# Unsplit transposes and paired K columns in the first stage, another order of the first Q results, and a buffer of its own for the last block's transposes

## The chip, the cores and the metric

The kernel runs on one core of one Trainium2 chip. The core has a matrix engine (TensorE, PE in the profile), three engines for elementwise work (VectorE or DVE, ScalarE or ACT, GpSimd or POOL), a queue engine (SyncE or SP) that issues most transfers, and 16 DMA engines. The metric is the device time of one execution in microseconds. Of the kernel before, three runs were timed; their median is 664.66 us (663.19 to 666.59).

## The reference

Both branches read the same normalised input `xn`, with 2048 tokens and 512 channels. One is attention with 32 heads of 16 channels, the other a feed-forward over the token axis.

```python
def _A_ref(x, wqkv, wo):                    # B, S, D = 1, 2048, 512
    H = 32; Dh = D // H
    qkv = (x @ wqkv).reshape(B, S, 3, H, Dh).transpose(2, 0, 3, 1, 4)
    q, k, v = qkv[0], qkv[1], qkv[2]
    p = softmax(einsum("bhqd,bhkd->bhqk", q, k) * Dh ** -0.5)
    o = einsum("bhqk,bhkd->bhqd", p, v)
    return o.transpose(0, 2, 1, 3).reshape(B, S, D) @ wo

def _B_ref(x, w1, b1, w2, b2):              # F = 1376
    h = layernorm(x)
    u = gelu(einsum("bsd,sf->bdf", h, w1) + b1)
    y = einsum("bdf,fs->bds", u, w2) + b2
    return y.transpose(0, 2, 1)

xn = layernorm(x)
return x + _A_ref(xn, A_wqkv, A_wo) + _B_ref(xn, B_w1, B_b1, B_w2, B_b2)
```

## The kernel before

**A schedule made on the host.** Python code builds one ordered list of instructions for each engine before anything runs (class `Sched`, line 170). `Sched.add` takes an instruction with the data that it reads and writes, finds what it depends on, and gives it a planned start from a planned duration (`occ`, how long it holds its engine; `lat`, until its result may be read). `plan` turns dependencies into semaphore waits and `emit` writes the lists out. So the durations in the code (`TABLE`, `occ`, `lat`) do nothing on the chip themselves; they decide the order.

**The work.** Attention is cut into 32 blocks (4 quarters of the queries times 8 sets of 4 heads), and each block into 16 groups, one for each 128 keys: 512 groups. A group has four score matmuls, one per head, each 32 rows high, so that they run side by side in the array (`score_mm`, line 675). Its exponentials are made in one of two ways. Either ScalarE does it, two tiles of 128x1024 per group (`exp_tile`, line 700), or VectorE and GpSimd do it: VectorE copies the four score banks out as 16-bit integers (`dve_first`, line 760), and two shifted planes are added by VectorE or GpSimd (`add_plane`, line 773; `add_plane_pool`, line 779). PV, the product with the values (`pv_mm`, line 707), takes one set of four matmuls for a ScalarE group and three for a VectorE group. After a block, its sums are copied out, the denominators go through DRAM and come back as reciprocals spread over the partitions in `denb`, and GpSimd multiplies (`chain_epi`, line 1279). The projections, the feed-forward and the output product fill the time between scores as "chains" of steps on one PSUM bank each.

**The dispatcher** (line 1947 on) walks through planned time, and at each free engine picks the next step. `pe_step` issues the scores of the next ScalarE tile when one of its two double banks is free, and otherwise a PV set, a chain step or a filler matmul on zeros (line 1815). Its thresholds come from `POLICY` (line 97), one row of 16 numbers for each 10 us of planned time: how long scores may wait for other work, when VectorE gets a group, how full a bank queue must be, a seed that varies some of these, and so on.

**Form of the matmuls.** `mm` (line 604) issues a matmul whole while `quad[0]` is false; from line 1942 on, when the dispatcher runs, it splits each into four pieces of 32 output rows. That holds for transposes too (`turn=True`, line 610), which multiply a tile by the identity.

**The first stage.** x is loaded tile by tile (16 tiles of 128 tokens), normalised, transposed (`transpose_mm`, line 794) and copied to `xnT` (`xnT_evac`, line 822). Tiles 0 to 3 are written out by hand (lines 844 to 878) with the first Q (`qt0_mm`, `qt_evac`) and K (`k_mm`, `k_evac`); the others come as chains `chain_tp`, `chain_k1`, `chain_k`, `chain_v`. K for the first heads is multiplied tile by tile, 128 columns each. The query tile `QT` exists twice (slot 0 and 1), masked by `qmask`, in pieces of 256, 128 and 128 columns.

**The end.** The last block does not go through DRAM. `tail_epilogue` (line 1979) transposes its sums in 32x32 blocks on VectorE into `denb`, takes reciprocals, multiplies, and transposes back into `otmp`; then TensorE adds the last part of the output product to four banks (`tail["steps"]`, line 1418, holds what each bank still needs), and ScalarE and VectorE copy the results out for the store.

Of the kernel before, what the change touches and what calls it, by code (L numbers as in the profile page):

```python
# [66 lines left out]
class Op:  # L67
# [31 lines left out]
    (85.0, 140.0, 500.0, -1, 0, 1300.0, 100.0, 0.1, 3, 4, 2, 8500.0, 0, 0.0, 1200.0, 0),  # L99
    (175.0, 80.0, 500.0, -1, 0, 2000.0, 0.0, 0.2, 1, 5, 2, 8500.0, 18089, 0.0, 700.0, 2),  # L100
    (130.0, 150.0, 300.0, -1, 0, 1300.0, 0.0, 0.05, 2, 3, 2, 7500.0, 0, 0.0, 1000.0, 2),
    (205.0, 170.0, 450.0, -1, 0, 1300.0, 0.0, 0.05, 2, 3, 2, 10500.0, 93902, 1.0, 1800.0, 1),
    (185.0, 120.0, 350.0, -1, 0, 1300.0, 100.0, 0.2, 3, 3, 2, 5500.0, 0, 1.0, 1000.0, 2),
    (85.0, 140.0, 350.0, -1, 1, 1300.0, 100.0, 0.05, 3, 4, 0.9, 8000.0, 0, 0.0, 900.0, 1),
    (110.0, 230.0, 250.0, -1, 0, 1300.0, 0.0, 0.1, 1, 5, 2, 7500.0, 0, 150.0, 1000.0, 0),
    (85.0, 170.0, 350.0, 1, 0, 1300.0, 0.0, 0.05, 1, 3, 2, 7500.0, 0, 0.0, 800.0, 2),
    (115.0, 140.0, 300.0, -1, 0, 1300.0, 0.0, 0.2, 2, 3, 2, 5500.0, 57197, 1.0, 1000.0, 1),
    (195.0, 230.0, 250.0, 1, 0, 900.0, 0.0, 0.2, 3, 3, 2, 9500.0, 7708, 0.0, 700.0, 2),
    (140.0, 90.0, 400.0, -1, 1, 2000.0, 0.0, 0.2, 2, 5, 2, 7000.0, 0, 150.0, 700.0, 1),
    (85.0, 160.0, 300.0, -1, 0, 1300.0, 100.0, 0.1, 1, 4, 2, 5500.0, 0, 1.0, 1000.0, 1),  # L110
    (205.0, 150.0, 500.0, -1, 0, 900.0, 0.0, 0.1, 2, 5, 2, 8000.0, 35383, 150.0, 800.0, 1),
    (105.0, 130.0, 450.0, -1, 0, 2000.0, 200.0, 0.1, 2, 5, 0.9, 7000.0, 0, 1.0, 1200.0, 2),
    (130.0, 150.0, 300.0, -1, 0, 1300.0, 0.0, 0.05, 2, 3, 2, 7500.0, 0, 0.0, 1000.0, 2),
    (135.0, 230.0, 500.0, -1, 0, 900.0, 0.0, 0.05, 3, 3, 2, 6500.0, 0, 0.0, 1200.0, 1),
    (135.0, 230.0, 500.0, -1, 0, 900.0, 0.0, 0.05, 3, 3, 2, 6500.0, 0, 0.0, 1200.0, 1),
    (110.0, 110.0, 400.0, 1, 0, 2000.0, 0.0, 0.2, 2, 4, 2, 5500.0, 0, 0.0, 900.0, 2),
    (110.0, 190.0, 300.0, 1, 0, 900.0, 0.0, 0.05, 2, 4, 2, 5500.0, 61002, 150.0, 1000.0, 1),
    (135.0, 90.0, 350.0, 1, 0, 2000.0, 100.0, 0.05, 2, 5, 0.9, 5500.0, 0, 1.0, 1100.0, 2),
    (135.0, 90.0, 350.0, 1, 0, 2000.0, 100.0, 0.05, 2, 5, 0.9, 5500.0, 0, 1.0, 1100.0, 2),
    (135.0, 90.0, 350.0, 1, 0, 2000.0, 100.0, 0.05, 2, 5, 0.9, 5500.0, 0, 1.0, 1100.0, 2),  # L120
    (190.0, 230.0, 300.0, -1, 0, 1300.0, 0.0, 0.05, 1, 3, 2, 8000.0, 78883, 1.0, 1000.0, 0),
    (200.0, 220.0, 350.0, 1, 0, 900.0, 0.0, 0.0, 1, 3, 2, 10500.0, 0, 0.0, 800.0, 1),
    (170.0, 80.0, 300.0, -1, 0, 2000.0, 0.0, 0.05, 1, 2, 2, 8000.0, 42439, 1.0, 700.0, 2),
    (140.0, 90.0, 300.0, -1, 0, 2000.0, 0.0, 0.0, 1, 3, 2, 8500.0, 0, 0.0, 800.0, 1),
    (110.0, 180.0, 200.0, -1, 1, 1300.0, 200.0, 0.2, 1, 4, 2, 7000.0, 96947, 150.0, 500.0, 1),
    (110.0, 180.0, 200.0, -1, 1, 1300.0, 200.0, 0.2, 1, 4, 2, 7000.0, 96947, 150.0, 500.0, 1),
    (110.0, 180.0, 200.0, -1, 1, 1300.0, 200.0, 0.2, 1, 4, 2, 7000.0, 96947, 150.0, 500.0, 1),
    (95.0, 80.0, 500.0, 1, 0, 900.0, 0.0, 0.2, 1, 3, 2, 9500.0, 12616, 0.0, 1000.0, 1),
    (105.0, 210.0, 300.0, -1, 0, 1300.0, 0.0, 0.05, 2, 3, 2, 5500.0, 30810, 1.0, 1200.0, 2),
    (145.0, 240.0, 200.0, -1, 0, 1300.0, 100.0, 0.2, 1, 3, 2, 6500.0, 0, 0.0, 1200.0, 2),  # L130
    (130.0, 150.0, 300.0, -1, 0, 1300.0, 0.0, 0.05, 2, 3, 2, 7500.0, 0, 0.0, 1000.0, 2),
    (185.0, 170.0, 250.0, -1, 0, 2000.0, 0.0, 0.05, 2, 3, 2, 7500.0, 39811, 0.0, 1100.0, 2),
    (150.0, 160.0, 300.0, 1, 0, 2000.0, 200.0, 0.05, 2, 2, 2, 7500.0, 28503, 0.0, 1000.0, 2),
    (155.0, 170.0, 500.0, -1, 0, 900.0, 100.0, 0.2, 1, 4, 0.9, 6500.0, 0, 0.0, 500.0, 2),
    (170.0, 210.0, 300.0, -1, 1, 1300.0, 0.0, 0.05, 2, 5, 0.9, 8000.0, 0, 0.0, 1100.0, 1),
    (170.0, 130.0, 200.0, -1, 1, 1300.0, 0.0, 0.2, 1, 3, 0.9, 8500.0, 63054, 150.0, 700.0, 2),
    (115.0, 90.0, 500.0, -1, 0, 1300.0, 0.0, 0.05, 3, 2, 2, 7500.0, 20828, 0.0, 1000.0, 2),
    (90.0, 60.0, 300.0, 1, 0, 1300.0, 100.0, 0.1, 3, 2, 2, 6500.0, 0, 1.0, 900.0, 2),
    (100.0, 130.0, 200.0, -1, 0, 2000.0, 200.0, 0.05, 3, 4, 2, 8500.0, 0, 0.0, 1000.0, 2),
    (155.0, 80.0, 400.0, -1, 0, 1300.0, 200.0, 0.05, 2, 4, 2, 7500.0, 89316, 150.0, 1100.0, 0),  # L140
    (140.0, 220.0, 400.0, 1, 0, 1300.0, 0.0, 0.0, 3, 3, 2, 5500.0, 14451, 0.0, 700.0, 2),
    (195.0, 240.0, 500.0, 1, 0, 900.0, 0.0, 0.05, 2, 2, 2, 9500.0, 53805, 0.0, 1200.0, 1),
    (185.0, 170.0, 250.0, -1, 1, 900.0, 100.0, 0.2, 2, 3, 0.9, 7000.0, 39296, 0.0, 700.0, 2),
    (95.0, 70.0, 300.0, -1, 0, 2000.0, 100.0, 0.0, 2, 5, 2, 5500.0, 46810, 0.0, 1000.0, 2),
    (95.0, 70.0, 300.0, -1, 0, 2000.0, 100.0, 0.0, 2, 5, 2, 5500.0, 46810, 0.0, 1000.0, 2),
    (150.0, 200.0, 350.0, 1, 1, 900.0, 0.0, 0.2, 2, 2, 0.9, 7000.0, 0, 1.0, 1000.0, 2),
    (85.0, 150.0, 350.0, -1, 1, 2000.0, 200.0, 0.0, 1, 2, 2, 6500.0, 0, 150.0, 1400.0, 2),
    (160.0, 200.0, 400.0, 1, 1, 1300.0, 0.0, 0.05, 1, 3, 0.9, 7000.0, 47180, 0.0, 1000.0, 2),
    (85.0, 160.0, 300.0, 1, 0, 2000.0, 0.0, 0.05, 2, 5, 2, 10500.0, 55416, 150.0, 500.0, 2),
    (90.0, 120.0, 200.0, -1, 1, 1300.0, 0.0, 0.05, 1, 5, 2, 9500.0, 73998, 0.0, 500.0, 2),  # L150
    (90.0, 120.0, 200.0, -1, 1, 1300.0, 0.0, 0.05, 1, 5, 2, 9500.0, 73998, 0.0, 500.0, 2),
    (140.0, 200.0, 300.0, 1, 0, 2000.0, 0.0, 0.2, 1, 2, 2, 5500.0, 69683, 0.0, 1000.0, 0),
    (185.0, 80.0, 500.0, 1, 1, 1300.0, 0.0, 0.05, 3, 5, 2, 5500.0, 8504, 0.0, 1100.0, 0),
    (185.0, 80.0, 500.0, 1, 1, 1300.0, 0.0, 0.05, 3, 5, 2, 5500.0, 8504, 0.0, 1100.0, 0),
    (185.0, 80.0, 500.0, 1, 1, 1300.0, 0.0, 0.05, 3, 5, 2, 5500.0, 8504, 0.0, 1100.0, 0),
    (125.0, 100.0, 500.0, -1, 0, 900.0, 100.0, 0.05, 2, 4, 2, 5500.0, 0, 0.0, 1400.0, 0),
    (130.0, 150.0, 300.0, -1, 0, 1300.0, 0.0, 0.05, 2, 3, 2, 7500.0, 0, 0.0, 1000.0, 2),
    (90.0, 220.0, 300.0, 1, 0, 1300.0, 200.0, 0.05, 1, 2, 2, 6500.0, 0, 0.0, 800.0, 2),
    (185.0, 70.0, 300.0, -1, 0, 1300.0, 200.0, 0.1, 1, 2, 2, 7000.0, 59958, 0.0, 1000.0, 2),
# [181 lines left out]
def bass_parallel_sum__softmax_full_mha__mixer_token_mlp__prompt_kernel(  # L341
# [18 lines left out]
    with ExitStack() as es:  # L360
# [62 lines left out]
        def T_DVE(n, div=1.0):  # L423
            return dict(occ=(n / div + 64.0) / 0.96, lat=(n / div + 64.0) / 0.96 + 141.0)
# [3 lines left out]
        def dma(q, dst, src, reads, writes, name="", noncontig=False, out_dma=False, lat=2500.0, move=150.0):  # L428
# [12 lines left out]
            return op  # L441

        NPRE = 4
        TABLE = 1283.0
        LAT_I, LAT_B = 4300.0, 3100.0


# [1665 lines left out]
```

## Time and profile before

| | |
|---|---|
| runs | 664.66 us median of three (663.19 to 666.59) |
| the profiled execution | 662.49 us, of which the span is 660.7 us |
| mean granted TensorE clock | 0.997 |
| busy: TensorE, ScalarE | 645.0 us (98%) each |
| busy: VectorE, GpSimd | 617.5 us (93%), 423.8 us (64%) |
| TensorE matmuls | 9124 |
| exponential tiles on ScalarE | 682 + 4 |
| the power on GpSimd (line 583) | 2.94 us, once |
| DMA traffic | 33.03 MB, mean 50 GB/s |

The span runs from the first to the last instruction. A timeline line gives start, length, engine, line, operation, output <- input with their shapes, how many instructions were merged, and in brackets the idle time of the engine before them with what ended it. `PEld` is the weight load, which overlaps matmuls. "issue" as a releaser means that nothing in the profile explains the wait. Where an engine's time is spent in a stage is read from a table of windows: busy time of each engine, then the granted clock, the share of DMA time and the rate.

### The profile page before, as it was taken

The page shows a single profiled execution, that of the slowest core. Times are in us where ns is not written, and L with a number is a line of the kernel's source. Part 1 is how long each engine was busy: PE and PEld are TensorE (multiplying, and loading weights), DVE is VectorE, ACT ScalarE, POOL GpSimd, SP SyncE. Part 2 cuts the span into 40 slices and gives each one's busy share as a digit, 9 for nine tenths or more (in the row PEclk, how much of TensorE's full clock was granted, in tenths as well). Part 3 has the DMA queues.
Part 4 walks back from the last instruction along what each step waited for, and adds up shares of the span by engine and source line. Part 5 has one row for each costly group of instructions (what it writes and reads, how often), then busy time and mean ns, then how long its engine had stood idle before and what let it go on. Part 6 is the DMA issues. An engine that isn't in the chain of part 4 may idle for free.

```text
span 660.7 us, 21188 instructions
## 1 busy us (share of the span) xinstructions
PE 645.0 (98%) x9124; PEld 191.7 (29%) x9124; DVE 617.5 (93%) x1062; ACT 645.0 (98%) x705; POOL 423.8 (64%) x292
## 2 busy tenths in 40 slices
PE   7999999999999999999999999999999999999997
PEld 4543333322222222222222222222222222222222
DVE  7888999999999999899989999999999999999997
ACT  7899999999999999999999999999999999999995
POOL 5530677665555646886738886876688776646762
PEclk9899999999999999999999999999999999999999
DMA  7015100021212212220112222122020031222101
GB/s 223 5 27 134 29 23 21 23 59 36 54 34 55 57 36 56 52 53 20 29 48 54 64 56 54 41 53 65 19 53 25 22 86 30 74 62 60 36 23 50
DMA packets 77004, 33.03 MB, mean 50 GB/s; under 512 B 61618, under 2 KB 72818, under 8 KB 76910
## 3 DMA queue, kind: packets, MB, share of 16 engines
q1 hardware_dynamic: 76478, 31.27, 19.2%
q8 instruction: 72, 1.18, 0.8%
q10 hardware_dynamic: 432, 0.39, 0.2%
q14 instruction: 22, 0.18, 0.1%
HBM read 26.08 MB, written 2.61 MB: 43 GB/s over the span
## 4 chain that ended last, share of the span: by engine, by line
ACT 60%; PE 33%; DVE 3%; DMA 1%; POOL 1%; issue 1%; POOLq 0%; SPq 0%; DVEq 0%
ACT pT L701 58%; PE ps L678 12%; PE ps L714 11%; PE ps L611 10%; ACT gT L1061 1%; PE ps L610 1%; ACT xn_sb L701 1%; POOL r L583 0%; DVE h_sb L587 0%; DVE w1blk L761 0%; DVE x_sb L769 0%; DVE xn_sb L774 0%; DMA x_sb<-in_A_x_dram 0%; DMA denb<-rec_scr 0%; DMA rec_scr<-den_s 0%
## 5 line engine op out<-in xcount | busy, mean ns | idle before, releaser
L701 ACT ACTIVATE pT<-ps 128x1024 bf16<-128x1024 f32 x682 | 627.8, 1134 | 4.0 <-PE ps L678 3.8
L678 PE MATMUL ps<-QT,KT 32*128 32x512 bf16 x2048 | 277.7, 385 | 6.5 <-ACT pT L701 4.6
L678 PEld LDWEIGHTS ps<-QT,KT 32*128 32x128 bf16 x2048 | 71.3, 91 | 279.3 <-ACT pT L701 262.9
L714 PE MATMUL ps<-pT,V 128*32 128x512 bf16 x1364 | 133.8, 389 | 0.5 <-DVE OT L1286 0.5
L761 DVE TENSOR_SCALAR x_sb<-ps 128x512 int16<-128x512 f32 x178 | 117.5, 683 | 8.1 <-PE ps L678 6.4
L761 DVE TENSOR_SCALAR xn_sb<-ps 128x512 int16<-128x512 f32 x120 | 78.3, 682 | 5.3 <-PE ps L678 4.7
L761 DVE TENSOR_SCALAR plx<-ps 128x512 int16<-128x512 f32 x110 | 72.5, 682 | 4.0 <-PE ps L678 3.5
L781 POOL TENSOR_TENSOR x_sb<-xn_sb,shift_w 128x1024 int32<-128x1024 int32 x18 | 33.9, 1890 | 41.1 <-PE ps L678 20.4
L761 DVE TENSOR_SCALAR xnT<-ps 128x512 int16<-128x512 f32 x84 | 55.6, 684 | 4.6 <-PE ps L678 3.7
L611 PE MATMUL ps<-h_sb,w1blk 128*32 128x512 bf16 x688 | 56.5, 384 | 0.0
L611 PE MATMUL ps<-gT,w2blk 128*32 128x512 bf16 (+1 forms) x704 | 55.5, 383 | 0.0
L714 PEld LDWEIGHTS ps<-pT,V 128*32 128x32 bf16 x1364 | 34.6, 94 | 64.1 <-issue 59.1
L761 DVE TENSOR_SCALAR wqkv_sb<-ps 128x512 int16<-128x512 f32 x72 | 47.3, 680 | 2.4 <-PE ps L678 1.6
L611 PE MATMUL ps<-xnT,wqkv_sb 128*32 128x512 bf16 (+2 forms) x680 | 42.8, 324 | 1.9 <-issue 1.5
L714 PE MATMUL ps<-x_sb,V 128*32 128x512 bf16 x400 | 39.1, 383 | 0.0
L761 DVE TENSOR_SCALAR w1blk<-ps 128x512 int16<-128x512 f32 x58 | 37.3, 681 | 1.7 <-PE ps L678 1.2
L781 POOL TENSOR_TENSOR x_sb<-plx,shift_w 128x1024 int32<-128x1024 int32 x15 | 28.2, 1891 | 15.1 <-DVE plx L761 6.0
L781 POOL TENSOR_TENSOR xn_sb<-x_sb,shift_w 128x1024 int32<-128x1024 int32 x15 | 28.4, 1893 | 9.1 <-DVE x_sb L769 3.8
L714 PE MATMUL ps<-xn_sb,V 128*32 128x512 bf16 x280 | 27.9, 383 | 0.0
L781 POOL TENSOR_TENSOR plx<-x_sb,shift_w 128x1024 int32<-128x1024 int32 x10 | 18.9, 1892 | 12.1 <-PE ps L678 7.8
L1323 POOL TENSOR_TENSOR oT<-OT,denb 128x512 bf16<-128x512 f32 x16 | 20.4, 1274 | 7.8 <-DVE wqkv_sb L774 7.8
L761 DVE TENSOR_SCALAR h_sb<-ps 128x512 int16<-128x512 f32 x36 | 23.5, 682 | 1.1 <-PE ps L678 1.0
(201 smaller groups left out, 871.6 us busy)
## 6 DMA issues: line engine op xcount, KB each, us to landing
denb<-rec_scr SPq DMA_DIRECT2D x124, 64.0 KB, 2.0
w1blk<-in_B_w_dram SPq DMA_DIRECT2D x10, 512.0 KB
w2blk<-in_B_w_dram SPq DMA_DIRECT2D x16, 320.0 KB, 3.5
xres<-in_A_x_dram SPq DMA_DIRECT2D x16, 128.0 KB, 2.3
QT<-qst SPq DMA_DIRECT2D x120, 16.0 KB, 1.8
out_dram<-osb SPq DMA_DIRECT2D x14, 128.0 KB, 1.8
wqkv_sb<-in_A_wqkv_dram SPq DMA_DIRECT2D x3, 384.0 KB, 7.7
x_sb<-in_A_x_dram SPq DMA_DIRECT2D x2, 512.0 KB, 6.5
```

Of the source, the lines that this page charges most:

```text
L610: return e.transpose(dst[a:b, :], lhsT[:, a:b], rhs, **pos)
L611: return e.matmul(dst[a:b, :], lhsT=lhsT[:, a:b], rhs=rhs, start=start, stop=stop, **pos)
L678: return sc.add("pe", lambda e: e.matmul(bank(bk), lhsT=KT[32 * r:32 * r + 32, T, 128 * kt:128 * (kt + 1)], rhs=QT[32 * r:32 * r + 32, slo ...
L701: return sc.add("act", lambda e: e.activation(pT_buf(buf), ps[:, slot * 1024:(slot + 1) * 1024], ACTF.Exp, scale=EXP_SCALE), reads=[("bank ...
L714: return sc.add("pe", lambda e: e.matmul(bank(PV_BANK)[32 * r:32 * r + 32, :], lhsT=vt_[:, off:off + 32], rhs=rhs, start=start, stop=stop, ...
L761: return sc.add("dve", lambda e: e.tensor_scalar(plane_i[pb][:, 512 * r:512 * (r + 1)], bank(bk), BIAS, 0.0, ALU.add, ALU.max), reads=[("b ...
L781: return sc.add("pool", lambda e: e.tensor_tensor(plane_w[pb], plane_w[pb0], shift_w[:, j:j + 1].broadcast_to([128, 1024]), ALU.add), read ...
L1061: op = sc.add("act", lambda e, m=m, f0=f0, f1=f1: e.activation(gT[0:m, f0:f1, :], gT[0:m, f0:f1, :], ACTF.Gelu_apprx_tanh), reads=[("gT", ...
L1323: op = sc.add("pool", lambda e: e.tensor_tensor(dst, OT32[:, eb, :], denb[:, :], ALU.mult), reads=[("OT32", eb)] + [("denb", r) for r in r ...
```

## The change

Five things are edited.

1. Transposes are always issued whole, also when the dispatcher runs. K for the first heads is multiplied for two tiles at once, 256 columns wide, in one chain step instead of two.
2. In the part written by hand, the transpose of tile 3 moves ahead of the first K product, all of slot 0's Q pieces come ahead of slot 1's first one, and VectorE takes three of the six pieces (ScalarE had all six).
3. The last block's transposes write into buffer 0 of `pT`, seen as 32-bit numbers, instead of `denb`. After the VectorE work of the last block is listed, all but the last pending TensorE step of each output bank are issued, ahead of the steps that wait for that VectorE work.
4. Planned durations are changed: the table load from 1283 to 1490 ns, the power on GpSimd from 2000 to 2900, small ScalarE evacuations to at least 240 or 245.
5. 60 rows of `POLICY` get other numbers.

```diff
 POLICY = [
     (130.0, 150.0, 300.0, -1, 0, 1300.0, 0.0, 0.05, 2, 3, 2, 7500.0, 0, 0.0, 1000.0, 2),
-    (85.0, 140.0, 500.0, -1, 0, 1300.0, 100.0, 0.1, 3, 4, 2, 8500.0, 0, 0.0, 1200.0, 0),
-    (175.0, 80.0, 500.0, -1, 0, 2000.0, 0.0, 0.2, 1, 5, 2, 8500.0, 18089, 0.0, 700.0, 2),
+    (90.0, 110.0, 300.0, -1, 0, 1300.0, 0.0, 0.1, 2, 2, 2, 5500.0, 0, 0.0, 500.0, 2),
+    (150.0, 80.0, 200.0, 1, 0, 900.0, 200.0, 0.1, 2, 2, 2, 9500.0, 3970, 0.0, 1100.0, 0),
...
-        TABLE = 1283.0
+        TABLE = 1490.0
...
-                          reads=[("r2",), ("mhalf",)], writes=[("r2",)], occ=2000, lat=2060)
+                          reads=[("r2",), ("mhalf",)], writes=[("r2",)], occ=2900, lat=2970)
...
-                              occ=64 + n / 1.2, lat=242 + n / 1.2)
+                              occ=max(240.0, 64 + n / 1.2) if n < 512 else 64 + n / 1.2, lat=242 + n / 1.2)
...
         def mm(dst, lhsT, rhs, start, stop, reads, writes, n=512, m=128, turn=False, name=None):
-            lat = 430.0 if n == 512 else 265.0
-            occ = 226.0 if n == 512 else 56.0
+            lat, occ, nm = {512: (430.0, 226.0, "q5"), 256: (320.0, 113.0, "q2"), 128: (265.0, 56.0, "q1")}[n]
...
-            if not quad[0]:
+            if not quad[0] or turn:
                 return sc.add("pe", lambda e: form(e, 0, m, {}), reads=reads, writes=writes, occ=occ, lat=lat, cfg="F")
...
-        def k_mm(t, bk, j):
+        def k_mm(t, bk, j, n=1):
             for ct in range(NCT):
-                op = proj_mm(bank(bk)[:, 128 * j:128 * (j + 1)], wqkv_sb[:, 1, ct, 0:128],
-                             xnT[:, t // 4, ct, 128 * (t % 4):128 * (t % 4) + 128], ct, [("wqkv", 1, 0), ("xnT", t)], bk, 128)
+                op = proj_mm(bank(bk)[:, 128 * j:128 * (j + n)], wqkv_sb[:, 1, ct, 0:128],
+                             xnT[:, t // 4, ct, 128 * (t % 4):128 * (t % 4 + n)], ct,
+                             [("wqkv", 1, 0)] + [("xnT", t + i) for i in range(n)], bk, 128 * n)
...
         qt0_mm(0, QB)
+        transpose_mm(3, 1, 0)
         k_mm(0, KB, 0)
-        transpose_mm(3, 1, 0)
+        xnT_evac(3, 1, 1, 0, "dve")
         k_evac(0, 1, KB, 0, "act")
-        xnT_evac(3, 1, 1, 0, "dve")
         qt0_mm(1, QB)
         qt_evac(0, QB, "act", 0, 256)
+        qt0_mm(2, 4)
+        qt_evac(0, 4, "dve", 256, 384, "QTh")
+        qt0_mm(3, 5)
+        qt_evac(0, 5, "act", 384, 512, "QTi")
+        k_mm(1, KB, 1)
         qt_evac(1, QB, "act", 0, 256)
-        qt0_mm(2, 4)
-        k_mm(1, KB, 1)
-        qt0_mm(3, 5)
         k_evac(1, 1, KB, 1)
-        qt_evac(0, 4, "act", 256, 384, "QTh")
-        qt_evac(0, 5, "act", 384, 512, "QTi")
-        qt_evac(1, 4, "act", 256, 384, "QTh")
-        qt_evac(1, 5, "act", 384, 512, "QTi")
+        qt_evac(1, 4, "dve", 256, 384, "QTh")
+        qt_evac(1, 5, "dve", 384, 512, "QTi")
...
-            c = Chain("k1", [Step("pe", lambda t=t: k_mm(t, 5, t - 2), 226) for t in (2, 3)]
+            c = Chain("k1", [Step("pe", lambda: k_mm(2, 5, 0, 2), 452)]
...
-            return Chain("k%d" % t, [Step("pe", lambda: k_mm(t, bk[0], 0), 226),
-                                     Step("pe", lambda: k_mm(t + 1, bk[0], 1), 226),
+            return Chain("k%d" % t, [Step("pe", lambda: k_mm(t, bk[0], 0, 2), 452),
...
-            dn = denb[:, :].rearrange("p (c m) -> p c m", m=32)
+            dt = pT[:, 0, :].bitcast(F32)
+            dn = dt.rearrange("p (c m) -> p c m", m=32)
...
-                sc.add("dve", lambda e, cols=cols: e.transpose(denb[:, cols], bank(PV_BANK)[:, cols]),
-                       reads=[("bank", PV_BANK)], writes=[dk] + ([("denb", r) for r in range(4)] if hf == 0 else []),
+                sc.add("dve", lambda e, cols=cols: e.transpose(dt[:, cols], bank(PV_BANK)[:, cols]),
+                       reads=[("bank", PV_BANK)], writes=[dk] + ([("pT", 0)] if hf == 0 else []),
...
+            for z in tail["steps"]:
+                while len(z) > 1:
+                    z.pop(0)[1]()
             for hf in range(2):
                 tr = sc.streams["dve"][hf - 2].end
```

## The prediction

> **What bounds the kernel now.** I read the page first (busy shares, the chain that ended last, the costliest groups), then ScalarE's timeline for gaps, then TensorE's timeline, the windows table and the DMA section around the one large gap, and last the timeline of the final 10 us.
>
> ```profile
> PE 645.0 (98%) x9124; PEld 191.7 (29%) x9124; DVE 617.5 (93%) x1062; ACT 645.0 (98%) x705; POOL 423.8 (64%) x292
> ...
> q8 instruction: 72, 1.18, 0.8%
> ...
> ACT 60%; PE 33%; DVE 3%; DMA 1%; POOL 1%; issue 1%; POOLq 0%; SPq 0%; DVEq 0%
> ...
> L701 ACT ACTIVATE pT<-ps 128x1024 bf16<-128x1024 f32 x682 | 627.8, 1134 | 4.0 <-PE ps L678 3.8
> ```
>
> ScalarE sets the end: 686 exponential tiles (682 here, 4 in a group of their own), and almost no wait. Near the end 14 of them took 13.03 us; less some 0.2 of the last one's overlapping write that is 0.917 us a tile. 686 × 0.917 = 629 of the 660.7 us. What is not exponentials is the way to the first tile (10.38), two table loads and GELU (7.6), the way from the last tile's end (652.46) to the end (8.2), and gaps. The largest gaps sit together:
>
> ```profile
> 8.54 1.87 ACT L639 ACTIVATE QT<-ps,qmask 128x256 bf16<-128x256 f32 x6 [0.17 <-PE ps L611]
> 10.38 6.52 ACT L701 ACTIVATE pT<-ps 128x1024 bf16<-128x1024 f32 x7
> 18.07 1.02 ACT L701 ACTIVATE pT<-ps 128x1024 bf16<-128x1024 f32 x1 [1.17 <-PE ps L678]
> 20.02 1.02 ACT L701 ACTIVATE pT<-ps 128x1024 bf16<-128x1024 f32 x1 [0.92 <-PE ps L678]
> 21.53 25.02 ACT L701 ACTIVATE pT<-ps 128x1024 bf16<-128x1024 f32 x27 [0.49 <-PE ps L678]
> ```
>
> At 0.917 a tile the eighth tile could start at 10.38 + 7 × 0.917 = 16.80, not 18.07 (1.27 lost); the ninth 1.04 earlier than it did, the tenth 0.59: 2.9 us in all. TensorE's timeline says why:
>
> ```profile
> 15.17 0.39 PE L678 MATMUL ps<-QT,KT 32*128 32x512 bf16 x2
> 17.08 0.41 PE L611 MATMUL ps<-xnT,wqkv_sb 128*32 128x128 bf16 x16 [1.52 <-issue]
> ```
>
> It stood still for 1.52 us and no semaphore released it. Its records up to there number 449; the instruction queue moves 16 KB a transfer, one per about 250 TensorE records, and its first transfer after the start begins at 14.57, 3.6 us after record 193 (256 before the stall) at 10.98, while later ones begin 0.2 to 1.1 us after the same point. In between the loads fill the DMA engines. I read it as code that came late. The windows table, cut at the steps of the granted clock, shows the after-effect (columns: span of the stretch, busy time of PE, PEld, DVE, ACT, POOL, granted clock, DMA share, GB/s):
>
> ```profile
> 7.70:11.12 3.42, 2.54 (x79) 2.06 (x80) 2.63 (x7) 2.92 (x9) 1.51 (x4) 1.00 1.01 332
> 11.12:14.53 3.41, 3.40 (x128) 1.87 (x116) 3.38 (x8) 3.41 (x5) 2.18 (x5) 1.00 1.05 329
> 14.53:17.94 3.41, 1.89 (x47) 0.91 (x42) 2.18 (x7) 2.38 (x3) 0.79 (x2) 1.00 0.12 35
> 17.94:21.36 3.42, 3.42 (x62) 1.61 (x60) 2.31 (x8) 2.05 (x2) 1.58 (x4) 0.50 0.02 5
> ```
>
> A stretch with PE busy 1.89 us of 3.41 is followed by one at half clock, one with 2.54 is not. So the 1.27 is the stall, the other 1.6 the half clock.
>
> The end:
>
> ```profile
> 652.78 0.40 PE L714 MATMUL ps<-wqkv_sb,V17b 128*32 128x512 bf16 x4
> 652.81 1.27 POOL L1323 TENSOR_TENSOR oT<-OT,denb 128x512 bf16<-128x512 f32 x1 [5.89 <-DVE wqkv_sb L774]
> 654.13 0.40 PE L611 MATMUL ps<-wo_pad,oT 128*32 128x512 bf16 x4 [0.52 <-POOL oT L1323]
> 654.21 0.78 DVE L1993 STREAM_TRANSPOSE denb<-ps 128x256 f32<-128x256 f32 x2 [1.48 <-POOL oT L1323]
> ```
>
> The last sum is complete at 653.2, but the transposes overwrite `denb`, which GpSimd's product for the block before still reads until 654.08.
>
> **Part by part**, against the profiled execution (662.49 us, of which 660.7 span and 1.8 around it; the median of the runs, 664.66, lies 2.2 above it).
>
> *Fewer instructions.* Transposes unsplit: 12 tiles × 4 × 4 pieces become 12 × 4, and the bias one 4 to 1: 147 matmuls less. K(0) in pairs: 7 chains × 32 become 7 × 16, 112 less. 259 matmuls and as many weight loads, 518 of some 18,250. Streaming time stays: 16 unsplit 128-column matmuls took 1.08 us at 8.12 (0.057 each after the latency), 32 pieces in fours 0.63 at 12.75 (the same 0.057 per four). Before the stall this drops 16 matmuls of K(2,3) and 24 of the transposes of tiles 4 and 5, 40 matmuls or 80 records. Those 80 now cover V(4), a score, a PV and V(5), 17.30 to 18.79 in the trace and about 1.2 us at full clock, so the code in hand lasts to about 16.8 instead of 15.56. If the late block arrives as now (first use 17.08; the transfer waited for the loads to drain, and those are unchanged), 0 to 0.75 us of stall stays, in which ScalarE still has a tile in hand, and the stretch keeps over 2.6 us of PE busy, more than the 2.54 that kept the clock. Gain 2.7, bounds 0 and 2.9.
>
> The Trainium skill (Runtime: NRT & Kernel Launch, Instruction fetch mechanics) describes both a TensorE store of 2048 instructions and one of only two 16 KiB blocks; the stall at record 449 agrees with the second. By the first the stall would not be code, and the sum would be 1.8 instead of 4.5.
>
> *Switching.* An unsplit transpose among split matmuls changes the array's form. The near row is score to PV: 0.32 between their starts where like follows like in 0.22, so 0.10 a switch. Six pairs of tiles × two switches = 1.2 us of TensorE at most, none where a score (which switches anyway) stands beside it. K as one step of 0.45 may push a score back by 0.22; V blocks of that size at 24.17 and 27.69 left ScalarE without a gap. That stage also holds two blocks of filler matmuls (13.21, 20.30) as cover. Cost 0.2, bounds 0 and 1.5. The Trainium skill (TensorEngine Tiling, Key Properties) states that a change of tiling mode drains the engine, which speaks against the edit; the 0.10 is that price as this trace has it, and all twelve would make the sum 3.5.
>
> *Start order.* ScalarE evacuates six pieces of Q from 8.54 to 10.41, and the first scores wait 0.76 for the fourth (slot 0's last). After: tile 3 is transposed ahead of K(0), about 0.2 earlier, slot 0 needs two pieces on ScalarE and one on VectorE, and slot 1 follows. From the rows: xnT(3) out by 8.55, its Q product to 9.0, its evacuation (0.37) to 9.4, scores, first tile at 9.85 instead of 10.38. Gain 0.5, bounds 0 and 0.8. VectorE takes three more pieces of some 0.3 us ahead of the statistics of tiles 4 to 6; who waits is K(4,5), first scored by the ninth tile near 17.2 and multiplied at 14.18 already, so 0.9 later is hidden by 2 us.
>
> *Planner's figures.* They change no instruction, only the order. One matters: the power on GpSimd is planned at 2000 and took 2940 ns. VectorE waits 0.60 for it at 38.56, is in the chain without a pause to 46.87, and ScalarE loses 0.62 at 48.09. With 2900 planned something else stands there. Gain 0.5, bounds 0 and 0.9. The others (table load, small evacuations) are off this chain: 0.
>
> *New table.* All 60 changed rows steer which groups go to VectorE, when TensorE leaves scores, and when filler runs. The page cannot price a row, but it prices the result: a group of four heads moved from ScalarE to VectorE saves two tiles, 1.83 us, and costs VectorE 4 × 0.60 plus some of its two planes, about 3.0. VectorE's busy time per 50 us lies between 45.5 and 48.6 over ten stretches, a spread of about 0.85 each, 3.1 over the run: one group, 1.8 us, either way. I take 0. VectorE's 43 us of idle time caps the gain: 9 groups would level it with ScalarE (16 us).
>
> *Last block.* Transposes into pT buffer 0, whose readers are done with the last PV, start at 653.2. From their start to the second output transpose's end is 2.07 us (654.21 to 656.28), so `otmp` is there 1.0 earlier. TensorE: 13 fours of 0.217 from 653.23 are 2.8, to 656.05; they ended at 657.27. The unblocked ones now go first and only the four `wo_pad`-`oT` wait for GpSimd's 654.08. Everything behind (two evacuations each on ScalarE and VectorE, the stores) follows. Gain 1.0, bounds 0 and 1.2.
>
> Sum: 2.7 + 0.5 + 0.5 + 1.0 − 0.2 = **4.5 us**: 658.0 for a profiled execution like this one, 660.2 for the median.
>
> **Rivals.**
> *The table packs VectorE fuller* (four groups more, 7.3 us on top): for it the 43 us idle; against it TensorE at 98%. 652.9.
> *The stall stays*: TensorE runs ahead with filler and uses the saved records up, the block comes later because it is asked for later, or the pause was not code. 16 KB on the instruction queue just before the resumption speaks against the last. 662.9.
> *The end is held elsewhere*: the product's own chain (its broadcast is issued at 648.53) lands later in the new order; the tail's 1.0 and the power's 0.5 are lost. 661.7.
> *Slower: the table gives groups back to ScalarE.* Place: the choice of group and free bank in the dispatcher; price 1.83 us each, without a wait to show for it. From (4.5 + 3.3) / 1.83 = 4.3 groups on it is slower; at five, 669.3 less the terms that hold: 664.66 − 4.5 + 9.2 = 669.3. For it: a chaotic list order; against: VectorE was 93% busy under a table of the same kind.
>
> **How the numbers follow.** Forecast 0.55, fuller 0.13, stall stays 0.12, end held 0.09, slower 0.11. The forecast's own range is 657.0 to 663.0 (one group either way and the terms' bounds). 0.5% is 3.3 us, about what a measurement of this kernel can tell from no change. Below 661.3 lie five sixths of the forecast, the fuller case and a third of the held end: 0.61; above 668.0 the slower case less a little: 0.10; between, 0.29. The range runs from the fuller case's near edge, 654.0, to 665.5, where the stall case ends with a group lost.
>
> **What would show it.** Right: no `issue` gap over 0.5 us on TensorE near 15 us, granted clock 1.00 there, first tile before 10.0, 259 fewer matmuls (filler aside), VectorE's transposes no longer released by GpSimd, about 686 tiles. Wrong: half clock in the first 25 us, a tile count off by more than 4, or new gaps on ScalarE in the first 40 us from switched transposes.

## The result, and the profile after

The changed kernel takes **657.39 us** (median of four runs, 657.22 to 657.74). Beside it the kernel before took 664.0 (four runs): a ratio of 0.9894, 95% interval 0.9866 to 0.9923. In a second set of runs on one chip it took 657.19 (six runs) against 662.81 (23 runs), ratio 0.992 (0.9897 to 0.9942). The forecast was 660.2, range 654.0 to 665.5; a gain of 4.5 was forecast, and 5 to 6.6 came. The profiled execution took 657.41 with a span of 655.6 (before 662.49 and 660.7).

Of the page, busy shares, instruction queue, chain, and the group of the exponential tiles (its last columns: idle time before them and what ended it):

```profile
PE 643.7 (98%) x8873; PEld 189.8 (29%) x8873; DVE 616.6 (94%) x1071; ACT 643.6 (98%) x702; POOL 424.2 (65%) x292
...
q8 instruction: 70, 1.15, 0.7%
...
ACT 76%; PE 19%; DVE 2%; DMA 1%; POOL 0%; issue 0%; DVEq 0%; POOLq 0%
...
L701 ACT ACTIVATE pT<-ps 128x1024 bf16<-128x1024 f32 x682 | 626.9, 1136 | 1.1 <-PE ps L678 0.9
```

ScalarE's idle time before these tiles fell from 4.0 to 1.1 us, and ScalarE's part of the chain rose from 60 to 76%. The tiles are 686 again. TensorE has 251 matmuls fewer: 259 by the edits, and eight more of filler. The start, in ScalarE's timeline and then TensorE's, around the place where TensorE had stood still:

```profile
8.58 1.20 ACT L639 ACTIVATE QT<-ps,qmask 128x256 bf16<-128x256 f32 x3
9.99 20.74 ACT L701 ACTIVATE pT<-ps 128x1024 bf16<-128x1024 f32 x22 [0.21 <-PE ps L678]
```

```profile
14.80 0.39 PE L678 MATMUL ps<-QT,KT 32*128 32x512 bf16 x2
15.12 0.62 PE L611 MATMUL ps<-xnT,wqkv_sb 128*32 128x256 bf16 x16
15.67 0.39 PE L678 MATMUL ps<-QT,KT 32*128 32x512 bf16 x2
15.99 0.63 PE L611 MATMUL ps<-wqkv_sb,xnT 128*32 128x128 bf16 x32
16.65 0.39 PE L678 MATMUL ps<-QT,KT 32*128 32x512 bf16 x2
```

Three Q evacuations stand on ScalarE instead of six; the first tile starts 0.39 earlier, and 22 stand in one row without a pause over 0.1 us between them. TensorE goes on without an `issue` gap, and K comes 256 columns wide in steps of 0.55. The windows of the granted clock, cut at its steps in this run (span, busy time of PE, PEld, DVE, ACT, POOL, granted clock, DMA share, GB/s):

```profile
13.18:16.59 3.41, 3.41 (x72) 1.64 (x70) 3.38 (x11) 3.41 (x5) 1.87 (x5) 1.00 0.45 147
16.59:20.01 3.42, 3.25 (x48) 1.41 (x44) 3.42 (x11) 3.42 (x4) 2.12 (x6) 1.00 0.03 5
```

Neither window is short of TensorE's work, and neither is at half clock; the kernel before had a window with 1.89 us of 3.41 and then one at half clock. The end:

```profile
648.30 1.29 POOL L1323 TENSOR_TENSOR oT<-OT,denb 128x512 bf16<-128x512 f32 x1 [7.03 <-DVE w1blk L774]
648.94 0.78 DVE L1994 STREAM_TRANSPOSE pT<-ps 128x256 f32<-128x256 f32 x2 [0.73 <-PE ps L714]
650.01 0.60 PE L611 MATMUL ps<-wo_pad,oT 128*32 128x512 bf16 x8
650.75 0.62 PE L611 MATMUL ps<-wo_pad,otmp 128*32 128x512 bf16 x8
```

VectorE's transposes now wait for TensorE's last sum, run beside GpSimd's product instead of behind it, and `wo_pad`-`oT` waits for nobody.

**Where the time went.** ScalarE sets the end, so the starts of its tiles account for the span. Each row below takes one profiled execution: the first tile's start; what distances over 1.1 us between two starts have above 0.917, up to 26 us and later (with their number in brackets; the one distance of 8.74 around GELU and its table load is left out); all the rest up to the last tile's start; from there to the end.

| kernel | first tile | lost to 26 us | lost later | rest | last tile to end | span |
|---|---|---|---|---|---|---|
| before | 10.38 | 2.91 | 2.80 (7) | 635.2 | 9.43 | 660.7 |
| after | 9.99 | 0.27 | 1.16 (2) | 635.7 | 8.48 | 655.6 |
| after, second profile | 10.13 | 0.27 | 0.58 (2) | 635.8 | 8.50 | 655.3 |

Before to after: 0.39 + 2.64 + 1.64 − 0.54 + 0.95 = 5.1. The rest lies between 635.2 and 635.8 in every kernel here with 686 tiles, so the experiments can be read in the other columns; delays too short to bring a distance over 1.1 stand in it.

### The profile page after: what moved, and what is told of

Its sections match the earlier page's. It is cut to its first block, busy times and chain, and to the rows that moved or that the text cites. A ratio compares the mean times of both kernels' runs of the same rounds, so it can differ in the third digit from the quotient of the medians.

```text
span 655.6 us, 20689 instructions
## 1 busy us (share of the span) xinstructions
PE 643.7 (98%) x8873; PEld 189.8 (29%) x8873; DVE 616.6 (94%) x1071; ACT 643.6 (98%) x702; POOL 424.2 (65%) x292
## 3 DMA queue, kind: packets, MB, share of 16 engines
q8 instruction: 70, 1.15, 0.7%
## 4 chain that ended last, share of the span: by engine, by line
ACT 76%; PE 19%; DVE 2%; DMA 1%; POOL 0%; issue 0%; DVEq 0%; POOLq 0%
ACT pT L701 74%; PE ps L678 7%; PE ps L714 7%; PE ps L611 5%; ACT gT L1062 1%; ACT xn_sb L701 1%; DMA den_s<-den_scr 0%; DVE stats L528 0%; DMA x_sb<-in_A_x_dram 0%; POOL mv L549 0%; DVE xn_sb L566 0%; DMA den_scr<-OT 0%; DVE x_sb L761 0%; ACT L701 0%; ACT L1062 0%
## 5 line engine op out<-in xcount | busy, mean ns | idle before, releaser
L761 DVE TENSOR_SCALAR x_sb<-ps 128x512 int16<-128x512 f32 x190 | 125.0, 684 | 7.8 <-PE ps L678 6.2
L761 DVE TENSOR_SCALAR xn_sb<-ps 128x512 int16<-128x512 f32 x140 | 92.6, 685 | 6.6 <-PE ps L678 5.3
L761 DVE TENSOR_SCALAR plx<-ps 128x512 int16<-128x512 f32 x104 | 68.5, 684 | 4.5 <-PE ps L678 3.8
L761 DVE TENSOR_SCALAR xnT<-ps 128x512 int16<-128x512 f32 x72 | 47.4, 685 | 2.2 <-PE ps L678 1.5
L714 PE MATMUL ps<-x_sb,V 128*32 128x512 bf16 x380 | 36.1, 383 | 0.0
L781 POOL TENSOR_TENSOR x_sb<-x_sb,shift_w 128x1024 int32<-128x1024 int32 x14 | 26.5, 1891 | 14.3 <-DVE x_sb L761 6.3
L781 POOL TENSOR_TENSOR x_sb<-xn_sb,shift_w 128x1024 int32<-128x1024 int32 x9 | 17.0, 1892 | 25.7 <-PE ps L678 18.3
L781 POOL TENSOR_TENSOR xn_sb<-x_sb,shift_w 128x1024 int32<-128x1024 int32 x13 | 24.5, 1893 | 7.6 <-DVE plx L774 2.8
L781 POOL TENSOR_TENSOR x_sb<-plx,shift_w 128x1024 int32<-128x1024 int32 x11 | 20.8, 1891 | 10.7 <-DVE plx L761 3.6
L761 DVE TENSOR_SCALAR h_sb<-ps 128x512 int16<-128x512 f32 x40 | 26.2, 685 | 1.4 <-PE ps L678 1.2
```

The source lines that it names most:

```text
L714: return sc.add("pe", lambda e: e.matmul(bank(PV_BANK)[32 * r:32 * r + 32, :], lhsT=vt_[:, off:off + 32], rhs=rhs, start=start, stop=stop, ...
L761: return sc.add("dve", lambda e: e.tensor_scalar(plane_i[pb][:, 512 * r:512 * (r + 1)], bank(bk), BIAS, 0.0, ALU.add, ALU.max), reads=[("b ...
L781: return sc.add("pool", lambda e: e.tensor_tensor(plane_w[pb], plane_w[pb0], shift_w[:, j:j + 1].broadcast_to([128, 1024]), ALU.add), read ...
```

## Experiments

"Planned order kept" means that every engine's list is that of the kernel named, instruction for instruction, except for what the diff says. The kernel before took 662.36 (35 runs) beside the first four, 662.81 (23) beside the next four, 661.37 (13) and 662.28 (11) beside the last two pairs. Two theories on the main term: the stall near 15.6 us is code that comes late, and fewer instructions put off the need for it; or it is something else (a data wait that the profile does not name, or the array's forms), which neither the count of instructions nor the loads would move.

**1. Transposes and K whole, in the order of before** (315 matmuls fewer, since all of the first heads' K is whole here).

```diff
+            if turn or name == "k0":
+                op = sc.add("pe", lambda e: form(e, 0, m, {}), reads=reads, writes=writes, occ=occ, lat=lat + 22.0, cfg="P")
...
+                return op
```

> Before, with its own planned order kept instruction for instruction; only the transposes of tiles 4 to 15 and the first heads' K products are issued whole instead of in four pieces (315 matmuls fewer). Theory (code arrives late behind the loads): the TensorE pause near 15.6 us shrinks to under 0.4, the granted clock stays 1.00 to 21 us, ScalarE's eighth to tenth tiles come 2.9 us earlier, and the end with them: 2.5 to 3 us less than before, about 661. Rival (the pause is something else, or the new table made the gain): pause and time as before, within 0.5 us. Rival (array-form switches cost): less than 2 us of the gain is left.

662.75 us (660.96 to 664.91), ratio 0.9983 (0.9954 to 1.0011). The stall is gone; ScalarE's timeline:

```profile
10.38 24.73 ACT L707 ACTIVATE pT<-ps 128x1024 bf16<-128x1024 f32 x26
35.28 10.19 ACT L707 ACTIVATE pT<-ps 128x1024 bf16<-128x1024 f32 x11 [0.17 <-PE ps L684]
```

Yet the median did not move, where 2.5 to 3 us had been expected; by the time alone the second rival, that switching eats the gain, came nearest. In the profile 7.42 us are lost after 26 us instead of 2.80: at 257.1 a tile comes 1.57 late (0.82 in the kernel before), and from 487.9 to 494.0 five tiles lose 3.8, because TensorE waited for VectorE there and this run pays for it with two windows at half clock:

```profile
484.15:487.56 3.41, 2.01 (x21) 0.54 (x17) 3.41 (x5) 2.71 (x3) 2.78 (x3) 1.00 0.10 27
487.56:490.97 3.41, 3.41 (x29) 0.61 (x26) 3.18 (x6) 2.45 (x3) 2.34 (x2) 0.50 0.03 5
```

So the edit removes the stall, as the theory says, and does not by itself make this order faster. The late tile near 257 can be followed back: GpSimd's product waits 3.62 us there, until the reciprocals from DRAM have landed, since SyncE's issue of the fourth of their transfers takes 1.70 us. In experiment 8, the other kernel with whole transposes in the old order, it takes 1.57; in the kernel before and in experiments 3, 4 (both kernels) and 6 it takes 0.42, and GpSimd waits 1.9 to 2.2 us. Why the issue takes longer is not shown. Two distances over 1.1 that only this order with whole transposes has, at 31.3 and 35.3 (0.25 and 0.29 lost), come of the switching of forms, as far as it can be told from the place; the net cost is less, for at the 50th tile this kernel is only 0.14 us behind that of experiment 3, which has neither the stall nor whole transposes.

**2. The changed kernel with the 259 matmuls put back**, planned order kept.

```diff
+            if quad[0] and turn:
+                for a in range(0, m, 32):
+                    op = sc.add("pe", lambda e, a=a: form(e, a, min(a + 32, m), dict(tile_position=(0, a))), reads=reads, writes=writes,
...
+                return op
...
+            if n == 2:
+                for i in range(2 * NCT):
+                    h, ct = divmod(i, NCT)
+                    for a in range(0, 128, 32):
...
```

> After, with its own planned order kept; only the 259 matmuls are put back (transposes in four pieces, paired K as two halves). Theory: the code in hand ends about 112 records earlier, near 15.1 us, the pause comes back with 0.7 to 1.5 us and perhaps the half clock behind it: 1 to 3 us slower than after (658.5 to 660.5) and a wider spread of the runs. Rival (the instruction count is nothing, the table is all): within 0.4 us of after.

659.5 us (658.05 to 666.09), ratio to before 0.9949 (0.9918 to 0.998): 2.3 above the changed kernel's 657.19, though each stands beside its own runs of before. The stall is back, with its after-effect; first TensorE's timeline, then the windows:

```profile
15.17 0.29 PE L816 MATMUL ps<-xnT,wqkv_sb 128*32 128x128 bf16 x8
16.85 0.52 PE L816 MATMUL ps<-xnT,wqkv_sb 128*32 128x128 bf16 x24 [1.38 <-issue]
```

```profile
14.64:18.05 3.41, 2.03 (x76) 1.09 (x68) 1.79 (x7) 2.23 (x4) 1.56 (x4) 1.00 0.17 52
18.05:21.46 3.41, 3.41 (x62) 1.24 (x50) 2.17 (x7) 2.75 (x3) 1.58 (x4) 0.50 0.00 0
```

4.23 us are lost up to 26 us. In the same order, the 259 matmuls make or unmake the stall; that it is their number and not their form, experiment 3 shows.

**3. The kernel before with three loads held back**: the remaining Wqkv columns are loaded after the second exponential tile. All instructions and their order stay.

```diff
-        ld_w(1, 1, 4, 16000, "sp")
+        ld_w(1, 1, 4, 16000, "sp", name="ld_late")
...
+        late = [o for o in sc.order if o.name == "ld_late"]
+        hold = [o for o in sc.streams["act"] if o.name == "exp"][1]
+        for o in late:
+            sc.order.remove(o)
+            o.deps.append(hold)
...
```

> Before, planned order kept, no instruction removed; only the three 384 KB loads of the remaining projection weights wait for the second exponential tile's end (12.3 us) instead of standing in the queue from 6.5 us. Theory: the code transfer that is asked for at 11.0 starts within about 1 us instead of 3.6, so the pause at 15.6 is gone with all instructions in place: 2.5 to 3 us less, about 661. Rival (the pause is not a transfer behind loads): pause stays 1.5 us, time within 0.5 us of before.

661.21 us (660.1 to 663.1), ratio 0.9973 (0.9947 to 1.0): 1.15 less than before, where 2.5 to 3 had been expected. No stall with all 9124 matmuls:

```profile
10.40 34.93 ACT L701 ACTIVATE pT<-ps 128x1024 bf16<-128x1024 f32 x37
```

The first transfer of the instruction queue after the start begins at 11.56 instead of 14.57. TensorE's record 449, the first behind the stall, lies 2.44 to 2.59 us behind that transfer's start in the six profiles that stall (14.57 and 17.08; 14.66, 17.10; 13.67, 16.26; 14.74, 17.33; 14.29, 16.84; 14.13, 16.58). In the changed kernel the transfer starts at 13.64 and the record is due at 16.39, 2.75 later: it passes by about 0.2 us, and by 0.4 in the second profile. This and experiment 2 settle that the stall is code held up behind the loads. They also show how thin the margin is: in the four profiles whose first 15 us are those of the kernel before, this transfer starts anywhere from 13.67 to 14.74, and in experiment 7 the record comes 2.53 us behind it, just in time.

**4. The last block alone**, on the kernel before, whole and by half. The first kernel takes the new buffer and the new order of TensorE's last steps (the loop over `tail["steps"]`); the second only the buffer.

```diff
+            dt = pT[:, 0, :].bitcast(F32)
+            dn = dt.rearrange("p (c m) -> p c m", m=32)
...
+            for z in tail["steps"]:
+                while len(z) > 1:
+                    z.pop(0)[1]()
```

> Before with the last block's part of the change alone (transposes into pT buffer 0, pending output steps ahead); everything before the last block is the same. Theory: VectorE's transposes start at 653.2 instead of 654.2, TensorE's last matmul ends 1.0 to 1.2 earlier: 1.0 us less than before, bounds 0.6 and 1.2. Rival (the end hangs on the block before's normaliser, through the product that the last output steps need): under 0.3 us.

> Kernel before with the last block's transposes in pT buffer 0 alone; the order of the eight out-projection chains and of the steps stays as it was. Theory (the wait for GpSimd's product was what held the transposes, and the order of the projections is a second, smaller wait): from the last tile's start to the end 9.0 to 9.2 us, where the kernel before has 9.43 and the version with both edits 8.66; transposes start about 1.0 earlier, but the matmuls of wo_pad and oT still stand first. Rival (the buffer is the whole gain): 8.5 to 8.7. A second rival (the order is the whole gain): 9.4.

Both edits: 661.57 us, ratio 0.9976 (0.9949 to 1.0003); from the last tile's start to the end 8.66 instead of 9.43. Buffer alone: 9.04. So the buffer is worth 0.39 and the order 0.38, and the changed kernel's 8.48 has 0.18 more. The time of the buffer alone does not show this: 663.66 us, ratio 1.003 (1.0005 to 1.0056). Seven of its ten runs were below clock 0.999, and all ten spent 2.0 to 2.8 us outside the span, where the other kernels spend some 1.8; why is open. In the kernel with both edits TensorE's step with `oT` still waits a little for GpSimd, and the last one for VectorE:

```profile
652.22 0.78 DVE L1994 STREAM_TRANSPOSE pT<-ps 128x256 f32<-128x256 f32 x2 [0.51 <-PE ps L714]
...
653.12 0.28 PEld L611 LDWEIGHTS ps<-wo_pad,oT 128*32 128x32 bf16 x8 [0.16 <-POOL oT L1323]
...
654.02 0.12 PEld L611 LDWEIGHTS ps<-wo_pad,otmp 128*32 128x32 bf16 x8 [0.63 <-DVE otmp L2008]
```

The same profile shows that the stall need not bring half clock. TensorE waits 1.51 us, up to 17.10 and mostly in a window that begins at 15.71, and the next window stays at full clock, so that 1.27 us are lost up to 26 us and not 2.9:

```profile
15.71:19.12 3.41, 2.02 (x76) 1.24 (x79) 1.92 (x8) 2.25 (x3) 0.97 (x3) 1.00 0.02 5
19.12:22.54 3.42, 3.38 (x86) 1.56 (x84) 3.42 (x10) 3.31 (x4) 2.35 (x7) 1.00 0.02 5
```

**5. The changed kernel once more**, unedited, on the chip of the next three.

> The changed kernel once more, beside the kernel before and the experiments on the same chip. Every theory: 657.4 us, a ratio of about 0.99 to the kernel before, and a spread under 2 us, because its start has no stall that a clock window could punish.

657.19 us (657.07 to 657.93, six runs), all at clock 1.00.

**6. The power in four pieces**, kernel before, planned order kept: a normalisation waits for its four columns only.

```diff
-            return sc.add("pool", lambda e: e.tensor_tensor(r2v, r2v, mhalf[:, :], ALU.pow),
+            for q in range(4):
+                op = sc.add("pool", lambda e, q=q: e.tensor_tensor(r2[:, 4 * q:4 * q + 4], r2[:, 4 * q:4 * q + 4],
+                                                                   mhalf[:, 0:4], ALU.pow),
+                            reads=[("r2",), ("mhalf",)], writes=[("r2q", q)], occ=500, lat=2060 - 500 * q)
...
-                          reads=[("xn", t), ("r2",)], writes=[("h", t)], occ=264, lat=405, two=True)
+                          reads=[("xn", t), ("r2q", t // 4)], writes=[("h", t)], occ=264, lat=405, two=True)
```

> Kernel before, planned order kept instruction for instruction; the power on GpSimd that closes the second layer norm's statistics is cut into four pieces of 4 columns, and a tile's normalisation waits for its own piece alone. If the power of 2940 ns is what VectorE and then ScalarE wait for near 38 to 48 us (theory): the 0.6 to 0.8 us gap of ScalarE near 44 to 48 is gone, the slip against the plan between tiles 30 and 50 falls from 1.2 to 0.3 or less, and the time is 0.6 to 1.2 us less than before. Rival (ScalarE's gap has another cause, or the pause only moves): gap and slip stay, 0 to 0.3 us. The stall at 15.6 us stays in both.

662.06 us (660.12 to 666.14), ratio 0.9998 (0.9976 to 1.002): the time cannot tell it from nothing. The trace can. This pause of ScalarE in the kernel before is gone:

```profile
48.09 12.28 ACT L701 ACTIVATE pT<-ps 128x1024 bf16<-128x1024 f32 x13 [0.62 <-PE ps L678]
```

What is lost between 26 and 50 us falls from 0.98 (41.9 and 48.1) to 0.50 (33.3 and 45.6). The mechanism holds, at 0.5 us. The stall did not stay as it was: TensorE waits 0.70 us, for a code transfer that starts at 13.67, and no half clock follows.

**7. The changed kernel with the old start order**, the rest of its order kept: tile 3 transposed behind K(0), all six Q pieces on ScalarE.

> Changed kernel with the start order of the kernel before (tile 3 transposed after K(0), all six Q pieces evacuated by ScalarE), everything after it in the changed kernel's order. Theory (the start order brings the first exponential tile forward and nothing later takes it back): first tile at 10.4 instead of 9.99, and 0.4 us more than the changed kernel. Rival (a later wait takes it back, so that the start order is worth nothing): first tile at 10.4, but the last tile's start within 0.1 us of the changed kernel's. No stall near 15 us in either; slip of the first 20 tiles below 1.6 us.

657.67 us (657.55 to 659.23). First tile at 10.41; 0.48 above the changed kernel on the same chip, and the last tile 0.50 later (647.32 and 646.82). Nothing later gives the start back: up to 290 us the tiles keep the same distances from the first one in all three profiles of the two kernels.

**8. Everything that the old order can carry**: the edits of 1, 4 (both) and 6 together on the kernel before. Without the new start, table and planned durations.

> Kernel before in its own planned order, with everything of the change that the old order can carry: transposes and K(0) whole (315 matmuls fewer), the last block's transposes in pT buffer 0 with the two orders of the changed kernel, the power in four pieces. Left out: the new start order, the new table and its order. Theory (the new table is worth nothing by itself; the chip only keeps closer to a plan of the same length): stall, tail and power together, 1.3 to 2.9 + 0.8 to 1.0 + 0.6 to 1.2, less 0.2 to 0.5 for what the table of before does with its plan being 0.4 us later: 658 to 659, within 1 us of the changed kernel plus its 0.4 for the start. Rival (the new order carries a gain of its own, by fewer waits in the middle): 660 or more, and the slip from tile 50 to the end is over 1 us larger than in the changed kernel.

660.04 us (659.52 to 661.64), ratio 0.9955 (0.9931 to 0.9979). This is 2.37 above experiment 7, on the same chip; between the two stand the table and the planned durations, that is, the order (and K in pairs, which the old order has tile by tile). The theory said at most 1; the rival is right. Both have 686 tiles, but here 3.92 us are lost after 26 us, in nine places; there 1.01, in two. The largest, from the timeline:

```profile
252.19 1.27 POOL L1336 TENSOR_TENSOR otmp<-OT,denb 128x512 bf16<-128x512 f32 x1 [3.43 <-DMA denb<-rec_scr]
253.43 1.89 POOL L794 TENSOR_TENSOR xn_sb<-plx,shift_w 128x1024 int32<-128x1024 int32 x1
...
255.37 0.40 PE L727 MATMUL ps<-xn_sb,V17b 128*32 128x512 bf16 x4 [1.35 <-POOL xn_sb L794]
```

GpSimd waits 3.43 us for the reciprocals' way through DRAM, a plane is queued behind that product, TensorE waits for the plane, and ScalarE loses 1.37. The changed kernel has one such place, where VectorE waits for the first half of the same round trip, the denominators, and ScalarE loses 0.87:

```profile
294.81 0.25 DVE L1301 RECIPROCAL den_s<-den_s 128x16 f32<-128x16 f32 x1 [0.85 <-DMA den_s<-den_scr]
```

In the second profile VectorE waits 0.27 there, and ScalarE loses 0.29.

**9. Tables in the wrong kernel**: the changed kernel with the old 60 rows, and the kernel before with the new ones.

> Changed kernel with the planner's table of the kernel before, so that the list order is made anew from that table. What the planner's own clock gives for it: end at 669.0 instead of 652.5, with 698 exponential tiles on ScalarE instead of 686. Theory (the chip follows the plan with a slip of about 1 us; the table is worth little between two tuned kernels, but much against a table tuned to another first stage): about 657.4 + 16.5 = 674, 672 to 676, slower than the kernel before by 1.5 to 2 per cent, with 698 tiles. Rival (the dispatcher's order matters little on the chip and the planner's clock overstates it): under 664, no slower than the kernel before.

> Kernel before with the new 60 rows of the planner's table and nothing else of the change (planned durations, first stage and last block as before). What the planner's own clock gives: end at 662.5 instead of 653.6, with 696 exponential tiles on ScalarE instead of 686. Theory (a table fits one plan only; tables are not better or worse by themselves): 8.9 us slower than the kernel before, 670 to 672, with 696 tiles. Rival (the new rows are better in themselves and carry part of the gain): at or below the kernel before, 662 or less.

674.0 us (672.77 to 675.38), 1.0177 of before (1.0151 to 1.0203), with 698 tiles; and 672.17 us (671.59 to 673.18), 1.0146 (1.0113 to 1.0179), with 696. Both fall within 1 us of where the planned end puts them, the second just outside its 670 to 672. Twelve tiles more are 11.0 of the first one's 16.8 us by the tile's 0.917; it also loses 6.9 after 26 us.

**10. The table altered once more**, for a planned end 0.46 earlier.

> Changed kernel with its table's rows altered further, so that the planner's clock gives 652.07 instead of 652.53 for the end; 686 tiles as before, the last one planned 0.02 us later, so all of the planned gain lies behind the last tile. Theory (the chip keeps the plan within its own scatter of waits): 0.46 less than the changed kernel, 656.7, but new waits for transfers in the middle, which the plan does not see and which cost between 0.3 and 0.9 us in two profiles of the changed kernel, can hide it: 656.5 to 657.6. Rival (the order of the changed kernel also happens to avoid waits that the planner does not see, and a new order loses that): 658 to 660.

657.54 us (657.14 to 661.34): no better than the changed kernel. From the last tile to the end it has 8.21 instead of 8.48, so 0.27 of the planned 0.46 came; after 26 us it loses 1.32, where the changed kernel lost 1.16 and 0.58. No version here is faster than the changed kernel.

The other profiles of the experiments, as in the table above:

| kernel | first tile | lost to 26 us | lost later | last tile to end | span |
|---|---|---|---|---|---|
| 1 whole | 10.38 | 0 | 7.42 (12) | 9.44 | 663.1 |
| 2 split again | 10.03 | 4.23 | 0.95 (2) | 8.49 | 659.5 |
| 3 late loads | 10.40 | 0 | 2.73 (8) | 9.43 | 658.3 |
| 4 last block | 10.42 | 1.27 | 3.18 (8) | 8.66 | 658.9 |
| 4 buffer alone | 10.36 | 4.41 | 6.55 (13) | 9.04 | 665.8 |
| 6 power | 10.38 | 0.46 | 2.40 (7) | 9.43 | 658.3 |
| 7 old start | 10.41 | 0.27 | 1.01 (2) | 8.49 | 655.8 |
| 8 all but table | 10.34 | 0 | 3.92 (9) | 8.65 | 658.4 |

## Why the prediction held, and where it did not

**Fewer instructions (forecast 2.7, bounds 0 and 2.9).** Right in mechanism, and in the two profiles right in size: 2.64 up to 26 us. The Trainium skill (Runtime: NRT & Kernel Launch, Instruction fetch mechanics) gives TensorE's store as 2048 instructions, and a few lines on an engine's store as two 16 KiB blocks; the stall that comes and goes with 40 matmuls at record 449 agrees with the second only. But the size was read from an execution in which half clock followed the stall, and that part is chance: of the six profiles with the stall, four have half clock behind it (one to five windows), two have none. In runs at clock 0.999 and 1.000 the term is about half or less: splitting again costs 1.3 (658.5 in experiment 2 against 657.2, on two chips), and without the stall the old order gains 0.18 (661.26 in experiment 1) or 0.45 (660.99 in experiment 3) on its 661.44 on that chip. One detail was wrong: I held the transfer at its old time. It started 0.93 earlier, about as far as it did in experiment 6 with the first stage unchanged, so the run and not the edit can account for it; none of the 0 to 0.75 us of stall that I had left open came.

**Switching (0.2).** Inside the bounds of 0 and 1.5. In the old order it is 0.14 net (experiment 1). In the changed kernel the scores come late for three tiles, at 20.23, 21.32 and 23.28, by 0.28, 0.18 and 0.14 us against the 0.90 of their neighbours, of which the table counts 0.27. The first of these scores stands behind a K step of two tiles:

```profile
19.25 0.62 PE L611 MATMUL ps<-xnT,wqkv_sb 128*32 128x256 bf16 x16
19.80 0.39 PE L678 MATMUL ps<-QT,KT 32*128 32x512 bf16 x2
```

How much of the 0.6 is the form, the step or the new order, no run separates.

**Start order (0.5).** 0.48 in the median, 0.39 and 0.25 at the first tile of the two profiles. The second one starts its first tile at 10.13, where I had said before 10.0.

**Planner's figures (0.5).** The pause at 48.09 is the power's, and 0.5 is what taking it away returns (experiment 6).

**New table (0, bounds 1.8 either way): the step that failed.** I priced the table by groups moved between ScalarE and VectorE, and as to those it is worth nothing: 686 tiles before and after. I did not price the order's waits, although the page showed them: ScalarE lost 2.80 us after 26 us, in seven places. Experiments 7 and 8 put the order, with the power already cured in both, at 2.4 us. Part of this only gives back what the whole transposes lose in the old order; against the kernel before itself, the columns show 1.64 for power and order together, where I had 0.5. A further 0.54 went the other way, in the rest. The runs at clock 0.999 and 1.000 on one chip show how the gain is divided: 661.3 before, 660.0 with all that the old order can carry, 657.6 with the new order, 657.2 with the new start. So fewer instructions, last block and power less switching, which I had at 4.0 together, brought 1.3, and the order, which I had at nothing, 2.3. That the sum came within 1.1 of the measured gain is in part luck, since these two errors go opposite ways.

**Last block (1.0).** 0.95: 0.39 the buffer, 0.38 the order, 0.18 with the new lists.

**The rivals.** The stall is gone, the end came 0.95 earlier and the tiles are 686, so neither the stall that stays, nor the end held elsewhere, nor the fuller table came. The slower one named the right place, a list order that gives groups back. In experiment 9 it does so, and the 12 tiles at its price are 11.0 of the 16.8 us; but it asks for a table that does not belong to the plan, and the change's table does.

**The base.** The forecast stands 2.8 above the result, though its gain was only 1.1 short of the 5.6 that one chip's runs show: 4.5 came off 664.66, the median of three runs, while 82 later runs of the kernel before have a median of 662.3. The mean granted clock of each run accounts for most of this:

| clock of the run | runs of before | median us |
|---|---|---|
| 0.999 and 1.000 | 44 | 661.4 |
| 0.996 to 0.998 | 24 | 663.1 |
| 0.994 and 0.995 | 7 | 664.1 |
| under 0.993 | 7 | 668.0 |

One window of 3.41 us at half clock is 1.7 us of 660, or 0.0026 of the mean clock. Every run has its own windows, and the same stall brings half clock in one run and not in the next. The ten runs of the changed kernel in the two sets all show 0.999 or 1.000, though it may not be safe from it: experiments 7 and 10, close to it, have one run each at 0.997 (659.23) and 0.991 (661.34). So its gain has two parts: 661.4 to 657.2, or 4.2 us, at full clock; and the 0 to 7 us that half-clock windows cost the kernel before. Experiment 4's buffer-alone kernel shows the lottery: 661.3 in its three runs at full clock, 667.9 in the profiled one at 0.987, with five windows at half clock in a row.

## What to carry to other kernels

When an engine stands still and no semaphore releases it, look at the instruction queue's transfers: the cure can be fewer instructions or a load issued later, and one run of each tells. Price the stall without the half clock that may follow it. In a hand-ordered schedule, price an order by the waits that it makes on the bound engine, not only by how much work it gives to whom, and after any edit make the table again for the new plan, since one that fits another plan cost 10 to 17 us here. Where one stall can throw the clock, take the base from many runs sorted by their granted clock before you subtract from it.

## What the runs showed of the hardware

- Code transfers are held up by data loads: the first one after the start, due near record 193 (10.98) by the pattern of the later ones, began at 14.57 beside the loads (13.15 to 15.26 in the other profiles) and at 11.56 with three loads held back.
- The granted clock is decided in windows of 3.41 us whose position differs from run to run (steps at 14.53 in one profile, 14.64 and 15.71 in others). Windows with PE busy 1.89, 2.01, 2.03, 2.15, 2.29 and 2.43 us (before, experiments 1, 2, 4 with the buffer alone, and the two of 9) were followed by half clock, windows with 2.02 and 2.06 (experiments 4 and 8) were not, so busy time alone does not decide it; what else does stays open.
- The way of the denominators through DRAM varies between executions of one program: VectorE waited 0.85 us for it in one profile of the changed kernel and 0.27 at the same place in the other.
